# Local and coarse attention with a gated feed-forward: the late operand first in each group of TensorE products

## The chip, the core and the metric

The kernel runs on one core of one Trainium2 chip. The metric is device time in microseconds (us) of the program. The core's engines are TensorE (PE for its products, PEld for its weight loads), VectorE (DVE), ScalarE (ACT), GpSimd (POOL) and SyncE (SP, which only issues transfers). Every engine runs its own queue in the order of the program, and semaphores tie the queues together.

## The reference

Inputs are q, k and v of 8 batches, 8 heads, 576 positions and 64 numbers a head. Two attentions are added, and the sum goes through a normed, gated feed-forward:

```python
q_d, k_d, v_d = means of q, k, v over groups of 4 positions     # 144 coarse positions
out_up = repeat(softmax(q_d k_d^T / 8) v_d, 4)                  # coarse attention
out_local = softmax(q k^T / 8, only |i - j| < 4) v              # a band of 7
x = (out_up + out_local) as 4608 tokens of 512
xn = x / sqrt(mean(x * x) + 1e-6) * rms_g
g = xn @ w_gate;  val = xn @ w_val                              # 512 -> 1536
out = (g * sigmoid(g) * val) @ w_out                            # 1536 -> 512
```

## The kernel before

The tokens are cut into 18 chunks of 256, counted here from 0. For each chunk the local attention is made on VectorE, ScalarE and GpSimd, the coarse part is added, the rows are normed and transposed on TensorE (L906), and the feed-forward runs on TensorE. To keep float32 precision, every operand of the feed-forward is held as a high and a low part (xh and xl, hs[:, 0] and hs[:, 1], and two parts of each weight), and a product is three TensorE products: high by high, high by low, low by high.

The feed-forward of a chunk goes over 12 slices f of 128 hidden columns. `first(f, 0)` and `first(f, 1)` (L975) make the gate and the value product, 12 TensorE products of 256 columns each, into one buffer ps_h. Then follow tanh (ACT, L982), gate and product (DVE, L985 and L990), the high part of the result (ACT, L996) and the low part (DVE or POOL, L999). `second(f)` (L1010) makes six products of 512 columns into the two buffers ps_o; its place is two slices behind `first`. The parts that come last are xl (L914, after xh) for the first products of a chunk, and the low part of hs for every `second`.

The coarse attention is done in 32 pieces, a batch and a pair of heads each. A piece computes scores (four small products, L499; the two heads, par 0 and 1, lie in rows 0 to 63 and 64 to 127 of TensorE), row peaks on DVE, powers on ACT, a transposition of the powers (`turn`, L527, eight small transposes), their copy back (ACT, L534), the products with the values (`values`, L541, eight), and a store. All of the chunk's small TensorE outputs share three buffers, ps_a. The coarse keys, queries and values are summed from four parts by transfers that POOL issues one after another (L362), into two buffers each of qk and vs; the first part of vs is loaded by SP (L358) once the values of an earlier pair of pieces are done. Chunk 4 is the first that needs batches 2 and 3, whose last piece is made while chunk 3 runs.

Two things set the order. Up to the start of chunk 3 a planner in the kernel (class Plan, with costs and due times) writes the order of all engines out, as far as its own clock reaches the due time of chunk 3 plus 10 us; this part is issued under `manual_schedule`. What comes after is emitted in program order, and the scheduler of the language is free to move instructions: each engine takes the one that is ready first by the scheduler's own clock, with the earlier one preferred. So a group of products may be cut up there, its ready products placed early, and other work between them.

In the trace one product of `scores` or `values` (float32 operands) is two records; a product of L975 or L1010 and a transpose is one.

## Time and profile before

| | |
|---|---|
| median of three runs | 1149.9 us (1147.46 to 1150.06) |
| span of the profiled execution, first to last instruction | 1144.2 us |
| median less span | 5.7 us |
| TensorE products busy | 1082.0 us, 95% of the span |
| VectorE busy | 927.7 us, 81% |
| ScalarE busy | 624.1 us, 55% |
| GpSimd busy | 255.7 us, 22% |
| mean granted TensorE clock | 0.977 |

A row of the timeline has the start of a run of like instructions, the time that it covers, the engine, the line, out<-in with shapes, and the number of records; idle time before it and what ended it stand in brackets. TensorE's products overlap in the pipeline, so the cost of a run is read as its start to the start of the next row, not as its own length. A row of the windows view has, for each engine, busy time and instructions, then the granted TensorE clock, the share of the transfer engines and GB/s.

### The profile page before, as it was taken

The numbers are of one execution on the slowest core, as the hardware profiler recorded it, in microseconds if no ns is written. First come the engines' busy times: TensorE is split into PE (matmuls) and PEld (weight loads), VectorE is DVE, ScalarE is ACT, GpSimd is POOL, SyncE is SP. The second block draws the span as 40 slices with busy tenths as digits, with TensorE's granted clock in tenths as the row PEclk, the third lists the DMA queues.
The fourth block names the chain that finished last, engine by engine and source line by source line (L and its number), as shares of the span: only waits on it lengthen the run. The fifth ranks groups of instructions, "written<-read, shape, count | busy, mean of one in ns | idle before, by whom it ended". The sixth has DMA issues, their size and how long they took to land.

```text
span 1144.2 us, 22238 instructions
## 1 busy us (share of the span) xinstructions
PE 1082.0 (95%) x8002; PEld 990.2 (87%) x8002; DVE 927.7 (81%) x1869; ACT 624.1 (55%) x2284; POOL 255.7 (22%) x317
## 2 busy tenths in 40 slices
PE   6883799999999899999999999999999999999998
PEld 4772698888899899999999999999999999999997
DVE  6787898778889989797979797979798989887432
ACT  1574673747392847474747474747475573837221
POOL 1554562334221211111111111101011020201000
PEclk9885999999999999999999999999999999999999
DMA  9985482446535353535263535222231313220000
GB/s 264 301 275 170 102 227 76 95 101 149 127 87 117 99 115 88 115 87 115 83 120 87 115 88 114 78 64 75 66 91 46 105 52 99 68 58 20 1 19 19
DMA packets 76815, 119.59 MB, mean 105 GB/s; under 512 B 26784, under 2 KB 36256, under 8 KB 76704
## 3 DMA queue, kind: packets, MB, share of 16 engines
q1 hardware_dynamic: 47520, 97.34, 28.8%
q0 software_dynamic: 8640, 15.93, 9.0%
q10 hardware_dynamic: 20544, 4.89, 2.0%
q8 instruction: 63, 1.03, 0.4%
q14 instruction: 48, 0.39, 0.1%
HBM read 106.33 MB, written 11.80 MB: 103 GB/s over the span
## 4 chain that ended last, share of the span: by engine, by line
PE 76%; DVE 9%; DMA 8%; ACT 3%; issue 3%; SPq 1%; POOL 1%; ACTq 0%; DVEq 0%; POOLq 0%
PE ps_h L975 46%; PE ps_o L1010 23%; PE ps_a L541 2%; DMA wg<-in_v_sum_dram 2%; DMA qk<-in_qk_sum_dram 2%; PE ps_a L499 2%; ACT prod L804 1%; DMA vs<-in_v_sum_dram 1%; PE ps_a L906 1%; DVE prod L757 1%; DVE o_sb L271 1%; PE ps_a L527 1%; DMA kv<-in_k_pad_dram 1%; DVE sc L761 1%; DMA up<-o_g 1%
## 5 line engine op out<-in xcount | busy, mean ns | idle before, releaser
L1010 PE MATMUL ps_o<-wo,hs 128*128 128x512 f32 x1296 | 356.0, 399 | 4.2 <-POOL hs L999 3.7
L975 PE MATMUL ps_h<-xh,wg 128*128 128x256 f32 x1728 | 348.2, 283 | 4.8 <-ACT xh L910 2.3
L975 PE MATMUL ps_h<-xh,wv 128*128 128x256 f32 x1728 | 343.0, 281 | 4.6 <-DVE sil L985 4.5
L975 PEld LDWEIGHTS ps_h<-xh,wg 128*128 128x128 f32 x1728 | 282.9, 190 | 14.2 <-ACT xh L910 3.0
L975 PEld LDWEIGHTS ps_h<-xh,wv 128*128 128x128 f32 x1728 | 281.9, 189 | 10.8 <-DVE sil L985 6.9
L804 ACT ACTIVATE prod<-kv,sc 128x64 f32<-128x64 f32 x1072 | 281.7, 408 | 13.0 <-DVE sc L795 4.8
L1010 PEld LDWEIGHTS ps_o<-wo,hs 128*128 128x128 f32 x1296 | 221.9, 188 | 41.4 <-POOL hs L999 6.2
L975 PE MATMUL ps_h<-xl,wg 128*128 128x256 f32 x864 | 244.8, 283 | 0.1
L975 PE MATMUL ps_h<-xl,wv 128*128 128x256 f32 x864 | 241.5, 280 | 0.0
L982 ACT ACTIVATE sil<-ps_h 128x256 f32<-128x256 f32 x216 | 82.9, 384 | 233.9 <-PE ps_h L975 208.8
L811 POOL TENSOR_TENSOR prod<-sc,kv 128x256 f32<-128x256 f32 x144 | 116.4, 843 | 397.4 <-DVE sc L795 175.4
L985 DVE SCALAR_TENSOR_TENSOR sil<-sil,ps_h 128x256 f32<-128x256 f32 x216 | 89.7, 415 | 103.1 <-ACT sil L982 91.0
L975 PEld LDWEIGHTS ps_h<-xl,wg 128*128 128x128 f32 x864 | 164.1, 190 | 6.9 <-issue 1.3
L975 PEld LDWEIGHTS ps_h<-xl,wv 128*128 128x128 f32 x864 | 163.6, 189 | 1.8
L996 ACT ACTIVATE hs<-sil 128x256 fp32r<-128x256 f32 x216 | 89.5, 416 | 136.9 <-DVE sil L990 122.4
L757 DVE TENSOR_TENSOR prod<-q_t,kv 128x896 f32<-128x896 f32 x140 | 151.7, 1086 | 5.6 <-DMA q_t<-in_q_band_dram 5.2
L830 DVE TENSOR_REDUCE x_t<-prod 128x128 f32<-128x896 f32 x128 | 136.8, 1077 | 23.6 <-ACT prod L804 16.4
L761 DVE TENSOR_REDUCE sc<-prod 128x14 f32<-128x896 f32 x144 | 154.5, 1077 | 0.4
L999 DVE TENSOR_TENSOR hs<-sil,hs 128x256 fp32r<-128x256 f32 x196 | 91.4, 466 | 29.5 <-ACT hs L996 29.2
L990 DVE SCALAR_TENSOR_TENSOR sil<-sil,ps_h 128x256 f32<-128x256 f32 x216 | 89.9, 416 | 8.1 <-PE ps_h L975 6.4
L362 POOL DMA_DIRECT2D qk<-in_qk_sum_dram x36 | 32.2, 895 | 187.3 <-DMA qk<-in_qk_sum_dram 111.8
L811 DVE TENSOR_TENSOR prod<-sc,kv 128x128 f32<-128x128 f32 (+2 forms) x144 | 69.5, 515 | 1.6 <-PE ps_o L826 0.8
(118 smaller groups left out, 984.3 us busy)
## 6 DMA issues: line engine op xcount, KB each, us to landing
kv<-in_k_pad_dram SPq DMA_DIRECT2D x72, 320.0 KB
kv<-in_v_pad_dram SPq DMA_DIRECT2D x72, 320.0 KB
qk<-in_qk_sum_dram POOLq DMA_DIRECT2D x36, 288.0 KB, 5.3
out_dram<-o_sb SPq DMA_DIRECT2D x36, 256.0 KB
q_t<-in_q_band_dram SPq DMA_DIRECT2D x70, 128.0 KB
vs<-in_v_sum_dram POOLq DMA_DIRECT2D x36, 144.0 KB, 3.5
qk<-in_qk_sum_dram SPq DMA_DIRECT2D x12, 288.0 KB
wo<-in_qk_sum_dram SPq DMA_DIRECT2D x2, 1152.0 KB
```

The source lines that it names most:

```text
L757: nc.vector.tensor_tensor(out=pr, in0=bcast(q[:, s0:s0 + 2], 2, NO), in1=window(k, s0), op=ALU.mult)
L761: nc.vector.tensor_reduce(out=self.sc[:, j, par, s0:s0 + 2], in_=self.pr[i], axis=AX.X, op=ALU.add,)
L804: nc.scalar.activation(out=self.pr[i][:, o, s], in_=self.v[j, par][:, s0 + s + o], func=AF.Copy, scale=p[:, s, o:o + 1],)
L811: (nc.vector if engine == "DVE" else nc.gpsimd).tensor_tensor(out=self.pr[i][:, a:b], in0=bcast(p[:, :, a:b].rearrange("p s o -> p o s"), ...
L830: nc.vector.tensor_reduce(out=self.x[j][:, s0:s0 + 2, par], in_=pr.rearrange("p o s d -> p s d o"), axis=AX.X, op=ALU.add,)
L975: nc.tensor.matmul(out=self.p[f][:, t], lhsT=wi(f)[:, 0, k], rhs=xi[:, k], start=(n == 0), stop=(n == 3 * KT - 1),)
L982: nc.scalar.activation(out=self.sil[f], in_=self.p[f][:, 0], func=AF.Tanh, scale=0.5)
L985: nc.vector.scalar_tensor_tensor(out=self.sil[f], in0=self.sil[f], scalar=1.0, in1=self.p[f][:, 0], op0=ALU.add, op1=ALU.mult,)
L990: nc.vector.scalar_tensor_tensor(out=self.sil[f], in0=self.sil[f], scalar=0.5, in1=self.p[f][:, 1], op0=ALU.mult, op1=ALU.mult,)
L996: nc.scalar.activation(out=self.hs[f][:, 0], in_=self.sil[f], func=AF.Copy)
L999: (nc.gpsimd if engine == "POOL" else nc.vector).tensor_tensor(out=self.hs[f][:, 1], in0=self.sil[f], in1=self.hs[f][:, 0], op=ALU.subtract,)
L1010: nc.tensor.matmul(out=self.o[j], lhsT=lhs[:, cols], rhs=rhs(f)[:, 0], start=(f == 0 and i == 0), stop=(f == NF - 1 and i == 2),)
```

## The change

Within each group of TensorE products the order is turned so that the operand that is ready last is used first: xl ahead of xh in `first`, the low part of hs ahead of the high part in `second` (with the second half of the rows first, but for the last slice), the second head ahead of the first in `scores` and `turn`, and the second half of rows first in `turn`. The products and their sums are the same, in another order. In the part that the scheduler orders, each score product of a piece is also tied behind the one before it on TensorE (`issue_after`, an edge of order alone with no semaphore); in the written-out part it is not.

```diff
             def high():
                 self.invert()
-                for par in range(2):
+                for par in (1, 0):
                     self.turn(par)
                     self.copy(par)
...
+            last = None
             for c in range(2):
-                for par in range(2):
+                for par in (1, 0):
                     rows = slice(par * D, (par + 1) * D)
-                    nc.tensor.matmul(
-                        out=self.s[par][:, c], lhsT=qs[rows, hp % 2, c * HALF:(c + 1) * HALF], rhs=ks[rows, hp % 2],
-                        start=True, stop=True,
-                    )
+                    with tc.issue_after(last) if last and loose else nullcontext():
+                        last = nc.tensor.matmul(
+                            out=self.s[par][:, c], lhsT=qs[rows, hp % 2, c * HALF:(c + 1) * HALF], rhs=ks[rows, hp % 2],
+                            start=True, stop=True,
+                        ).ins
...
         def turn(self, par):
-            for kc in range(2):
-                for c in range(2):
+            for c in (1, 0):
+                for kc in range(2):
...
-                for wi, xi in ((w[0], self.att.xh), (w[0], self.att.xl), (w[1], self.att.xh)):
+                for wi, xi in ((w[0], self.att.xl), (w[0], self.att.xh), (w[1], self.att.xh)):
...
-            for j in range(2):
+            for j in (0, 1) if f == NF - 1 else (1, 0):
                 cols = slice(j * P, (j + 1) * P)
-                for i, (lhs, rhs) in enumerate(((hh, wo[0]), (hh, wo[1]), (hl, wo[0]))):
+                for i, (lhs, rhs) in enumerate(((hl, wo[0]), (hh, wo[0]), (hh, wo[1]))):
...
     with tc.manual_schedule():
         plan.run(due[FIRST] + 10)
+    loose.append(True)
     plan.run()
```

The lines shift by three or four: L499 becomes L502, L527 L530, L541 L544, L975 L978, L1010 L1013. The written-out part keeps its order of groups on every engine; in the rest the scheduler comes to another order, at three kinds of places above all. In the rows wo and wg stand for parts of the weights, hs for the hidden result, a_g for the powers of a coarse piece.

TensorE, the scores of one coarse piece in one of the chunks 6 to 11 (the same in each of the six). Before:

```order
L1010 MATMUL ps_o<-wo_2_1577,hs 128x512
L499 MATMUL ps_a<-qk 72x144 x2
L1010 MATMUL ps_o<-wo_2_1576,hs 128x512 x2
L975 MATMUL ps_h<-xh,wg_0_408 128x256
L499 MATMUL ps_a<-qk 72x144 x2
L975 MATMUL ps_h<-xl,wg_0_408 128x256
L975 MATMUL ps_h<-xh,wg_0_409 128x256
```

Now:

```order
L1013 MATMUL ps_o<-wo_1_1478,hs 128x512
L502 MATMUL ps_a<-qk 72x144
L1013 MATMUL ps_o<-wo_2_1576,hs 128x512 x2
L1013 MATMUL ps_o<-wo_2_1577,hs 128x512
L1013 MATMUL ps_o<-wo_2_1576,hs 128x512 x2
L1013 MATMUL ps_o<-wo_2_1577,hs 128x512
L502 MATMUL ps_a<-qk 72x144 x3
L978 MATMUL ps_h<-xl,wg_0_408 128x256
```

The piece was cut into two and two score products, and is cut into one and three. In two more pieces from chunk 4 on, two and two become four in a row.

TensorE, the transposes of the powers of one piece, in the same chunk. Before:

```order
L975 MATMUL ps_h<-xh,wg_0_408 128x256
L527 MATMUL ps_a<-ident_sb,a_g 72x72
L1010 MATMUL ps_o<-wo_2_1576,hs 128x512 x2
L527 MATMUL ps_a<-ident_sb,a_g 72x72 x4
L975 MATMUL ps_h<-xl,wg_0_408 128x256
L527 MATMUL ps_a<-ident_sb,a_g 72x72 x3
L975 MATMUL ps_h<-xh,wg_0_409 128x256
```

Now:

```order
L1013 MATMUL ps_o<-wo_2_1577,hs 128x512
L978 MATMUL ps_h<-xl,wv_0_415 128x256
L978 MATMUL ps_h<-xh,wv_0_415 128x256
L530 MATMUL ps_a<-ident_sb,a_g 72x72 x8
L978 MATMUL ps_h<-xh,wv_0_416 128x256
L978 MATMUL ps_h<-xl,wv_0_415 128x256
```

Eight transposes stand in one run. From chunk 4 on there were 41 runs of L527 for 16 pieces, and there are 16.

TensorE, the value products (L541, now L544) of a piece shortly before chunk 3, after which SP may load the next vs. Before:

```order
L1010 MATMUL ps_o<-wo_0_441,hs 128x512
L541 MATMUL ps_a<-vs,a_g 72x64 x4
L975 MATMUL ps_h<-xh,wg_1_1220 128x256
L975 MATMUL ps_h<-xl,wg_1_1220 128x256
L975 MATMUL ps_h<-xh,wg_1_1221 128x256
L541 MATMUL ps_a<-vs,a_g 72x64 x3
L1010 MATMUL ps_o<-wo_0_440,hs 128x512 x2
L541 MATMUL ps_a<-vs,a_g 72x64
```

Now:

```order
L1013 MATMUL ps_o<-wo_0_440,hs 128x512 x2
L1013 MATMUL ps_o<-wo_0_441,hs 128x512
L544 MATMUL ps_a<-vs,a_g 72x64 x8
L978 MATMUL ps_h<-xl,wg_1_1220 128x256
L978 MATMUL ps_h<-xh,wg_1_1220 128x256
L978 MATMUL ps_h<-xh,wg_1_1221 128x256
```

The eight value products stand together. Between the scores of the piece before and the last of these products, 75 products of L975 and 18 of L1010 stood before; now 72 and 12 do. On SP the load of vs (L358) moves from behind a load of q_t and one of kv to ahead of them. From chunk 4 on, the values of one piece in each of seven chunks are also followed at once by a piece's scores, with one product of L1010 between them before.

More of the change, by code (lines that the diff above doesn't have):

```diff
@@ L1 @@
 import itertools
-from contextlib import ExitStack
+from contextlib import ExitStack, nullcontext
 import concourse.bass as bass
@@ L431, in add_v @@
             )
+    loose = []
     used = {"wg": [], "wv": [], "wo": []}
```

## The prediction

> **What bounds the kernel now.** I read the page's busy shares first, then busy time by stretches, to see whether TensorE (PE) bounds every stage or an average hides one where it waits.
>
> ```profile
> span 1144.2 us, 22238 instructions
> ...
> L1010 PE MATMUL ps_o<-wo,hs 128*128 128x512 f32 x1296 | 356.0, 399 | 4.2 <-POOL hs L999 3.7
> ```
>
> ```profile
> 300.00:400.00 100.00, 95.80 (x707) 87.36 (x706) 88.57 (x180) 60.23 (x238) 23.97 (x37) 0.98 0.42 100
> 400.00:500.00 100.00, 100.00 (x753) 91.97 (x753) 86.44 (x189) 59.19 (x229) 21.25 (x27) 1.00 0.42 98
> 1000.00:1050.00 50.00, 50.00 (x363) 46.93 (x363) 44.07 (x95) 28.74 (x111) 5.73 (x8) 1.00 0.16 48
> ```
>
> The columns behind the first are PE, PEld, DVE, ACT and POOL, then the granted clock. From 400 us on PE has no idle time; the last two rows are the first and nearly the last such stretch. So there a wait can't be removed, only PE's own cost; DVE, at 86 to 88 of each 100, runs beside it with some room. Before 400 us PE idles a little and other chains set the starts of chunks. The same shows in the last row of the first fence: over the whole program PE waited 4.2 us ahead of its 1296 second products, so beginning such groups with the late operand has little to save.
>
> What a chunk of products costs is read from the chain of waits, where the last chunk repeats every 4.12 us:
>
> ```profile
> 1104.23 2.75 PE ps_h L975 x24
> 1108.35 2.75 PE ps_h L975 x24
> ```
>
> A slice is 24 products of 2.75/24 = 0.115 us and six of (4.12 - 2.75)/6 = 0.23 us. Between products of these two kinds a change costs nothing. Whatever a row takes beyond 0.115 and 0.23 us a product is the price of the small products between.
>
> **The change, part by part.** The number of products stays. What moves is where the small ones stand, so I price a break between kinds.
>
> Scores (PE's timeline; one piece cut into one and three, then one whole, then one cut into two and two):
>
> ```profile
> 327.27 0.46 PE L499 MATMUL ps_a<-qk 64*72 64x144 f32 x2
> 327.67 0.73 PE L541 MATMUL ps_a<-vs,a_g 72*72 72x64 f32 x8
> 328.33 0.71 PE L499 MATMUL ps_a<-qk 64*72 64x144 f32 x6
> 328.96 0.38 PE L975 MATMUL ps_h<-xh,wg 128*128 128x256 f32 x1
> ...
> 509.25 0.48 PE L1010 MATMUL ps_o<-wo,hs 128*128 128x512 f32 x1
> 509.66 0.71 PE L499 MATMUL ps_a<-qk 64*72 64x144 f32 x8
> 510.31 0.72 PE L1010 MATMUL ps_o<-wo,hs 128*128 128x512 f32 x2
> ...
> 547.54 0.85 PE L1010 MATMUL ps_o<-wo,hs 128*128 128x512 f32 x3
> 548.32 0.71 PE L499 MATMUL ps_a<-qk 64*72 64x144 f32 x4
> 548.96 0.73 PE L1010 MATMUL ps_o<-wo,hs 128*128 128x512 f32 x2
> 549.52 0.28 PE L975 MATMUL ps_h<-xh,wg 128*128 128x256 f32 x1
> 549.73 0.71 PE L499 MATMUL ps_a<-qk 64*72 64x144 f32 x4
> 550.37 0.39 PE L975 MATMUL ps_h<-xl,wg 128*128 128x256 f32 x1
> 550.59 0.40 PE L975 MATMUL ps_h<-xh,wg 128*128 128x256 f32 x2
> ```
>
> Half a piece takes 0.64 us from its start to the next row (548.32 to 548.96, 549.73 to 550.37), and a whole piece 0.65: the two heads run side by side when they alternate, and one after the other when each half is one head's. Around each run the product before takes about 0.09 us more (547.54 to 548.32 is 0.78 for three, against 0.69) and the one behind about 0.10 more (550.37 to 550.59 is 0.22). So two and two costs 2 x (0.64 + 0.19) = 1.66, whole 0.65 + 0.19 = 0.84. One and three is 0.40 + 0.63 with two such borders, 1.41. The order now has, from chunk 4 on, six pieces at one and three where two and two stood: 6 x 0.25 = 1.5 us. Of the two pieces that become whole, the one in chunk 5 gives 0.82; the one at the start of chunk 4 is told below. Sum 2.3 us. The bounds: a whole piece's price for the six (4.9 + 0.8 = 5.7 us), or the old price (0.8). I take 2.3, since one and three stands in the trace.
>
> Transposes:
>
> ```profile
> 385.82 0.66 PE L527 MATMUL ps_a<-ident_sb,a_g 72*72 72x72 f32 x8
> 386.29 0.36 PE L975 MATMUL ps_h<-xl,wg 128*128 128x256 f32 x1
> ...
> 558.57 0.41 PE L527 MATMUL ps_a<-ident_sb,a_g 72*72 72x72 f32 x4
> 558.79 0.36 PE L975 MATMUL ps_h<-xl,wg 128*128 128x256 f32 x1
> 558.99 0.35 PE L527 MATMUL ps_a<-ident_sb,a_g 72*72 72x72 f32 x3
> 559.15 0.36 PE L975 MATMUL ps_h<-xh,wg 128*128 128x256 f32 x1
> 559.35 0.28 PE L975 MATMUL ps_h<-xh,wv 128*128 128x256 f32 x1
> ```
>
> Four take 0.22 us, three 0.16, eight 0.47, and the product behind any run takes 0.20 instead of 0.115. If four and four replaced eight: 0.44 + one more 0.085, against 0.47, so a break costs 0.055 us. 41 runs become 16: 25 x 0.055 = 1.4 us. That the scores follow the values at once saves little: the lone L1010 at 509.25 took 0.41, 0.18 too much, and that goes, but a border between the two small kinds comes (0.09 on 327.67 to 328.33); 7 x 0.05 = 0.3. From chunk 4 to the end PE's work thus falls by 2.3 + 1.4 + 0.3 = 4.0 us.
>
> Late operand first, where PE does wait. At the start of chunk 4:
>
> ```profile
> 374.76 0.71 PE L499 MATMUL ps_a<-qk 64*72 64x144 f32 x4
> 377.08 0.62 PE L975 MATMUL ps_h<-xh,wg 128*128 128x256 f32 x3 [1.62 <-ACT xh L910]
> 378.26 0.68 PE L499 MATMUL ps_a<-qk 64*72 64x144 f32 x4 [0.56 <-DVE xl L914]
> 378.87 0.55 PE L975 MATMUL ps_h<-xl,wg 128*128 128x256 f32 x1
> ```
>
> Now all four scores need the buffer that xl's first half (DVE) frees at about 378.2, and the first L975 needs xl. Half the scores had run in idle time at 374.76, and three L975 at 377.08. The scores then take the same 0.6 us from 378.2, whole, and the three L975 come behind: 3 x 0.115, a loss of 0.3 us, and this piece's 0.82 is not gained. Behind the waiting products stands all of PE, but ACT and DVE work on the next values meanwhile. In the written-out part the groups that wait for the low part of hs lose the two products that ran ahead of it, 2 x 0.23 = 0.46 us each; the whole wait before L1010 there is the 4.2 us above, and later waits take such a shift up. I count zero, bound 0.9 (two groups). xl, needed one product earlier, costs 0.1 us at most elsewhere.
>
> The chain into chunk 3 (two rows of the chain of waits, then the norm on DVE's timeline):
>
> ```profile
> 293.44 0.14 PE ps_a L541 x2
> ...
> 293.59 4.49 DMA vs<-in_v_sum_dram
> ```
>
> ```profile
> 311.98 1.29 DVE L894 TENSOR_TENSOR x_t<-x_t,rinv 128x512 f32<-128x512 f32 x2 [2.63 <-POOL rinv L890]
> ```
>
> The last value products release SP's load of vs, POOL adds three parts behind it, each waiting for the one before, and only then makes the root that the norm of chunk 3 waits for. These value products now have 3 x 0.115 + 6 x 0.23 = 1.7 us less of products ahead of them and some breaks fewer, about 1.9 us. SP's q_t and kv move behind vs and are wanted later. DVE had idled 2.63 us here, so the norm can come 1.9 us earlier; PE meets it, as 4 fewer products (0.8 us) stand ahead of that transposition. Whether chunk 4 starts earlier by as much hangs on DVE's queue, which works between the two norms (its order there hardly changes), and on the values of the last piece of batch 3, which move some 2 us back. I take 1.5 of the 1.9; bounds 0 and 2.2.
>
> Sum: -4.0 + 0.3 - 1.5 = -5.2 us. The profiled span becomes 1144.2 - 5.2 = 1139.0, and as the median of the runs lies 5.7 us above the span, the time becomes 1149.9 - 5.2 = 1144.7 us.
>
> **A rule against it.** PE's clock fell to half at the start of chunk 4:
>
> ```profile
> 378.00:380.00 2.00, 1.74 (x9) 1.58 (x10) 1.59 (x3) 2.00 (x10) 0.01 (x1) 0.73 0.77 294
> 380.00:382.00 2.00, 2.00 (x12) 2.00 (x11) 2.00 (x5) 2.00 (x10) 1.01 (x1) 0.50 0.00 0
> 382.00:384.00 2.00, 2.00 (x17) 2.00 (x17) 1.97 (x4) 2.00 (x11) 1.20 (x1) 0.91 0.62 168
> ```
>
> That is 2 x (0.27 + 0.50 + 0.09) = 1.7 us lost after the idle time from 375 to 378. The change leaves PE with nothing between 374.8 and 378.2, so it will fall again; a second one, at chunk 3, would cost 1.7 us, and none at all would give 1.7 back. The Trainium skill, "TensorE: Matmul & The Clock Gate", Part 1 (The HAM clock gate), says that the clock halves after an idle window of some 3.4 us that runs freely, and comes back after a busy one. By that rule which gap is caught is a matter of phase; the trace agrees with the length, about 3.4 us between 378.9 and 382.4, as an estimate from the three rows.
>
> **The rivals.** (1) The forecast, 1144.7; its own range 1143 to 1146.4. 58%. (2) Chunk 4 follows early and the clock isn't halved, or the six cut pieces cost less: 1.7 to 2.4 us more, 1142.5. 9%. (3) PE's saving comes, but the early chain gives nothing and a second clock drop costs 1.7: -4.0 + 0.3 + 1.7 = -2.0, 1147.9. For it: the values of chunk 4's last piece come later. Against it: DVE's 2.63 us of idle time. 18%. (4) DVE sets the period of chunks 4 to 11, so that a shorter PE gains nothing: only chunk 3's 1.5 us less 0.3 remains, 1148.7. For it: 88.57 of 100 busy at 300 to 400; against it: PE without idle time in 400 to 500, where DVE idles 13.6. 9%. (5) Slower: a group that begins with the late operand holds all of PE, where two products (0.46 us) used to run ahead of the low part of hs. It decides once 11 groups lose 0.46 (5.2 us) and 19 make it slower by over 0.3%; if one in four of the 168 groups from chunk 4 on did, 42 x 0.46 = 19.3 us, the time would be 1164. Against it stands the tail, where no other engine is late:
>
> ```profile
> 1131.80 0.38 ACT L982 ACTIVATE sil<-ps_h 128x256 f32<-128x256 f32 x1 [2.38 <-PE ps_h L975]
> 1133.57 0.42 DVE L999 TENSOR_TENSOR hs<-sil,hs 128x256 fp32r<-128x256 f32 x1 [0.48 <-ACT hs L996]
> ```
>
> From tanh to low part is 2.2 us, and the group stands two slices, 8.2 us, behind; DVE's backlog must reach 6 us. 4%. (6) The scores don't run side by side in the new order of heads: term one is lost, and ten whole pieces cost 0.4 more: 1144.7 + 2.3 + 4 = 1151. Against it: the six records of three at 328.33 take 0.63, as four of one head would. 2%.
>
> **How the numbers follow.** A measurement here tells about 0.3%, 3.4 us, from no change. Below 1146.5 lie (1), (2) and a little of (3): 0.70. Within: the rest of (3), (4) and most of (6): 0.25. Slower: (5) and a bad end of (6): 0.05. The range from 1140.5 to 1149.5 holds (1) to (4); its lower end is 1144.7 less 1.7 for the clock and 2.5 of the term of the scores, its upper end the case in which nothing but the transposes' 1.4 us is left, plus a us.
>
> **What would show it.** Scores in rows of x2 and x6 records at 0.4 and 0.63 us, transposes in rows of x8; the period of chunks 6 to 11 shorter by 0.5 us; PE without idle time from 400 us on; the norm of chunk 3 before 311 us and the first transposition of chunk 4 near 372. It is wrong if PE shows waits ahead of L1013 or L978 after 400 us, or if the norm of chunk 3 stays where it was.

## The result and the profile after

The changed kernel took 1139.6 us (median of four executions, 1136.23 to 1143.23), 0.9921 of the kernel before with a 95% interval of 0.9895 to 0.9947: 10.2 us less by the medians and 9.1 by the ratio, where 5.2 were forecast. The median lies 0.9 us below the lower end of the range; by the ratio the time is 0.9921 x 1149.9 = 1140.8 us, just inside it. A second comparison (experiment 10) gave 1139.88 us and 0.9933, 0.9905 to 0.9961. In one of the six executions of experiment 11 the mean granted clock was 0.559 in place of 0.970 to 0.974, and it took 1771.34 us; its ratio below is worked out from the other five.

The page and the stretches of the changed kernel, to be read as those of before:

```profile
span 1134.4 us, 22266 instructions
...
L1013 PE MATMUL ps_o<-wo,hs 128*128 128x512 f32 x1296 | 336.4, 396 | 7.2 <-POOL hs L1002 5.8
```

```profile
400.00:500.00 100.00, 100.00 (x773) 92.70 (x772) 88.41 (x195) 61.53 (x239) 22.89 (x27) 1.00 0.42 99
```

PE still has no idle time from 400 us on, but the stretch holds 773 records where it held 753. Ahead of the second products PE waits 7.2 us in place of 4.2, all of it before 314 us. The two profiled executions are fast ones of their kernels, with spans 5.7 and 5.2 us below the medians, so their difference can stand beside that of the medians.

To see where the time went, I take the first transposition of chunks 3, 6, 12 and 17 on PE's timeline. Before, then after:

```profile
312.81 1.23 PE L906 MATMUL ps_a<-ident_sb,x_t 128*128 128x128 f32 x8 [0.88 <-DVE x_t L894]
...
485.00 1.04 PE L906 MATMUL ps_a<-ident_sb,x_t 128*128 128x128 f32 x8
...
828.18 1.03 PE L906 MATMUL ps_a<-ident_sb,x_t 128*128 128x128 f32 x8
...
1082.60 1.04 PE L906 MATMUL ps_a<-ident_sb,x_t 128*128 128x128 f32 x8
```

```profile
311.51 1.04 PE L909 MATMUL ps_a<-ident_sb,x_t 128*128 128x128 f32 x8
...
480.71 1.04 PE L909 MATMUL ps_a<-ident_sb,x_t 128*128 128x128 f32 x8
...
819.35 1.03 PE L909 MATMUL ps_a<-ident_sb,x_t 128*128 128x128 f32 x8
...
1073.01 1.03 PE L909 MATMUL ps_a<-ident_sb,x_t 128*128 128x128 f32 x8
```

1.3 us are won up to chunk 3, 3.0 in chunks 3 to 5, 4.5 in chunks 6 to 11, 0.8 in chunks 12 to 16 and 0.2 behind, together the 9.8 us between the spans. The 0.8 is the surprise: chunks 12 to 16 hold no coarse piece, and PE has no idle time there.

The small products stand as the order said (scores of one piece, then transposes):

```profile
542.38 0.46 PE L502 MATMUL ps_a<-qk 64*72 64x144 f32 x2
542.77 1.66 PE L1013 MATMUL ps_o<-wo,hs 128*128 128x512 f32 x6
544.36 0.71 PE L502 MATMUL ps_a<-qk 64*72 64x144 f32 x6
545.00 0.38 PE L978 MATMUL ps_h<-xl,wg 128*128 128x256 f32 x1
...
553.87 0.66 PE L530 MATMUL ps_a<-ident_sb,a_g 72*72 72x72 f32 x8
```

One and three take 0.39 and 0.64 us. The norm of chunk 3, a piece of the chain of waits that leads to it, and the start of chunk 4 (before, then after):

```profile
310.15 1.29 DVE L897 TENSOR_TENSOR x_t<-x_t,rinv 128x512 f32<-128x512 f32 x2
```

```profile
305.39 0.09 DVE rinv L877
```

```profile
373.60 1.23 PE L906 MATMUL ps_a<-ident_sb,x_t 128*128 128x128 f32 x8 [0.74 <-DVE x_t L894]
```

```profile
371.71 0.46 PE L502 MATMUL ps_a<-qk 64*72 64x144 f32 x2
375.09 0.68 PE L502 MATMUL ps_a<-qk 64*72 64x144 f32 x6 [2.92 <-DVE xl L917]
```

```profile
376.00:378.00 2.00, 2.00 (x13) 2.00 (x12) 1.93 (x6) 2.00 (x11) 0.30 (x1) 0.59 0.05 18
378.00:380.00 2.00, 2.00 (x12) 2.00 (x11) 1.97 (x4) 2.00 (x11) 1.46 (x2) 0.55 0.52 134
```

The norm starts 1.8 us earlier (311.98 before), but not by the path that led to it before. There POOL gave out its last transfer of vs at 306.87 and began the root behind it at 307.70. Now that transfer goes out at 303.7, 3.2 us earlier, and the first step of the root on POOL (305.55) waits for a row of DVE, the 305.39 above. At chunk 4 the wait for the norm (0.74 us at 373.60) is gone; PE waits once, for xl, 2.92 us, and the clock falls afterwards as it did before: 2 x (0.41 + 0.45) = 1.7 us lost.

### The profile page after: what moved, and what is told of

Read it like the earlier page. It is cut to its first block, busy times and chain, and to the rows that moved or that the text cites. A ratio compares the mean times of both kernels' runs of the same rounds, so it can differ in the third digit from the quotient of the medians.

```text
span 1134.4 us, 22266 instructions
## 1 busy us (share of the span) xinstructions
PE 1067.8 (94%) x8002; PEld 982.7 (87%) x8002; DVE 921.6 (81%) x1869; ACT 622.5 (55%) x2284; POOL 261.3 (23%) x317
## 4 chain that ended last, share of the span: by engine, by line
PE 82%; DVE 7%; DMA 6%; issue 2%; ACT 2%; SPq 1%; POOL 1%; ACTq 0%; DVEq 0%; POOLq 0%
PE ps_h L978 49%; PE ps_o L1013 24%; PE ps_a L544 2%; DMA qk<-in_qk_sum_dram 2%; DMA wg<-in_v_sum_dram 2%; PE ps_a L502 2%; PE ps_a L909 1%; PE ps_a L530 1%; DVE prod L760 1%; DVE o_sb L271 1%; ACT up_t L858 1%; PE ps_o L829 1%; DVE sc L764 1%; SPq L396 1%; DVE wg L295 0%
## 5 line engine op out<-in xcount | busy, mean ns | idle before, releaser
L1013 PE MATMUL ps_o<-wo,hs 128*128 128x512 f32 x1296 | 336.4, 396 | 7.2 <-POOL hs L1002 5.8
L978 PE MATMUL ps_h<-xh,wg 128*128 128x256 f32 x1728 | 315.9, 279 | 1.7 <-DVE wg L295 1.7
L978 PE MATMUL ps_h<-xh,wv 128*128 128x256 f32 x1728 | 315.7, 279 | 0.0
L978 PEld LDWEIGHTS ps_h<-xh,wg 128*128 128x128 f32 x1728 | 266.9, 189 | 6.3 <-DVE wg L295 1.9
L1013 PEld LDWEIGHTS ps_o<-wo,hs 128*128 128x128 f32 x1296 | 228.4, 188 | 50.0 <-POOL hs L1002 8.0
L978 PEld LDWEIGHTS ps_h<-xh,wv 128*128 128x128 f32 x1728 | 266.7, 189 | 3.4
L978 PE MATMUL ps_h<-xl,wg 128*128 128x256 f32 x864 | 246.0, 285 | 1.7 <-DVE xl L917 1.4
L978 PE MATMUL ps_h<-xl,wv 128*128 128x256 f32 x864 | 242.7, 281 | 3.6 <-DVE sil L988 3.4
L814 POOL TENSOR_TENSOR prod<-sc,kv 128x256 f32<-128x256 f32 x144 | 119.0, 856 | 384.9 <-DVE sc L798 147.8
L978 PEld LDWEIGHTS ps_h<-xl,wv 128*128 128x128 f32 x864 | 163.6, 189 | 7.8 <-DVE sil L988 5.5
L978 PEld LDWEIGHTS ps_h<-xl,wg 128*128 128x128 f32 x864 | 163.5, 189 | 7.4 <-DVE xl L917 2.2
L1002 DVE TENSOR_TENSOR hs<-sil,hs 128x256 fp32r<-128x256 f32 x196 | 87.6, 448 | 21.2 <-ACT hs L999 20.9
```

The lines of the kernel that those rows point to most:

```text
L814: (nc.vector if engine == "DVE" else nc.gpsimd).tensor_tensor(out=self.pr[i][:, a:b], in0=bcast(p[:, :, a:b].rearrange("p s o -> p o s"), ...
L978: nc.tensor.matmul(out=self.p[f][:, t], lhsT=wi(f)[:, 0, k], rhs=xi[:, k], start=(n == 0), stop=(n == 3 * KT - 1),)
L1002: (nc.gpsimd if engine == "POOL" else nc.vector).tensor_tensor(out=self.hs[f][:, 1], in0=self.sil[f], in1=self.hs[f][:, 0], op=ALU.subtract,)
L1013: nc.tensor.matmul(out=self.o[j], lhsT=lhs[:, cols], rhs=rhs(f)[:, 0], start=(f == 0 and i == 0), stop=(f == NF - 1 and i == 2),)
```

## The experiments

Executions of one kernel differ by several us (the kernel before ran between 1142.6 and 1157.9 us beside these runs), but nearly all of that comes about before chunk 6, as far as three profiled executions of one order show (the change, experiments 8 and 10). So I read each run by parts. The table is worked out from the starts of PE's records: the time from the first transposition of chunk 0 to that of chunk 3, of chunk 3 to 6, 6 to 12 and 12 to 17; then for chunks 6 to 11 the mean distance from a 256-column product to the next product inside a run, and what is left of the stretch when 1728 and 432 products are taken off at their own mean distances (small products and borders).

| kernel | median us | ratio to before [95%] | 0-2 | 3-5 | 6-11 | 12-16 | distance ns | small, borders |
|---|---|---|---|---|---|---|---|---|
| before | | | 206.8 | 172.2 | 343.18 | 254.42 | 116.2 | 42.7 |
| the change | 1139.6 | 0.9921 [0.9895, 0.9947] | 204.6 | 169.2 | 338.64 | 253.66 | 115.3 | 39.9 |
| 1 coarse parts | 1142.5 | 0.9938 [0.9914, 0.9962] | 207.8 | 171.9 | 338.84 | 254.40 | 115.5 | 39.8 |
| 2 order of products | 1144.1 | 0.9954 [0.9935, 0.9973] | 211.0 | 172.3 | 339.21 | 253.67 | 114.4 | 41.9 |
| 3 free part only | 1139.5 | 0.9914 [0.9888, 0.9940] | 206.3 | 169.2 | 338.64 | 253.66 | 115.3 | 39.8 |
| 4 no queue of scores | 1142.8 | 0.9939 [0.9918, 0.9960] | 208.8 | 171.8 | 339.01 | 253.66 | 114.7 | 41.4 |
| 5 scores as a block | 1161.5 | 1.0124 [1.0099, 1.0148] | 206.6 | 183.5 | 344.35 | 253.66 | 114.7 | 46.7 |
| 6 xl first | 1148.6 | 0.9995 [0.9974, 1.0016] | 207.0 | 171.6 | 341.90 | 254.37 | 115.5 | 42.7 |
| 7 hl first | 1142.0 | 0.9964 [0.9943, 0.9985] | 209.2 | 171.8 | 339.05 | 253.77 | 114.4 | 41.9 |
| 8 the change's order, products alone behind it | | | 210.8 | 169.8 | 338.64 | 253.66 | 115.3 | 39.9 |
| 9 scores behind products | 1142.4 | 0.9960 [0.9938, 0.9982] | 212.0 | 171.2 | 335.04 | 253.66 | 115.3 | 36.4 |
| 10 the change again | 1139.9 | 0.9933 [0.9905, 0.9961] | 205.6 | 170.1 | 338.64 | 253.66 | 115.3 | 39.8 |
| 11 behind, from chunk 6 on | 1136.1 | 0.9875 [0.9840, 0.9911] | 205.6 | 169.9 | 335.04 | 253.66 | 115.3 | 36.3 |

### 1. The coarse parts alone

The changed kernel, with the products of L978 and L1013 in their old order:

```diff
-                for wi, xi in ((w[0], self.att.xl), (w[0], self.att.xh), (w[1], self.att.xh)):
+                for wi, xi in ((w[0], self.att.xh), (w[0], self.att.xl), (w[1], self.att.xh)):
...
-            for j in (0, 1) if f == NF - 1 else (1, 0):
+            for j in range(2):
-                for i, (lhs, rhs) in enumerate(((hl, wo[0]), (hh, wo[0]), (hh, wo[1]))):
+                for i, (lhs, rhs) in enumerate(((hh, wo[0]), (hh, wo[1]), (hl, wo[0]))):
```

> The change with the old order of products: only the coarse pieces' scores (second head first, queued behind each other) and their transpositions (rows outermost, second head first) are changed; L978's groups begin with xh and L1013's with hh as before. Theory A (the prediction: what is gained in chunks 6 to 11 are small products and their borders, and the small products do not need the new order of the groups): chunks 6 to 11 together 2.3 to 2.9 us shorter than before, the products' spacing inside a run at 116.2 ns as before, chunks 12 to 16 at 50.91 us each as before, the start of chunk 3 at 312.8 as before, and 1145.5 to 1146.5 us in all. Theory B (the shorter spacing of the products comes from calmer small products and not from the order in a group): also the spacing falls to about 115.3 ns, chunks 12 to 16 fall to 50.8, and the time is near 1143.5.

```profile
486.26 1.04 PE L909 MATMUL ps_a<-ident_sb,x_t 128*128 128x128 f32 x8
...
825.10 1.04 PE L909 MATMUL ps_a<-ident_sb,x_t 128*128 128x128 f32 x8
...
1079.51 1.04 PE L909 MATMUL ps_a<-ident_sb,x_t 128*128 128x128 f32 x8
```

Chunks 6 to 11 gave 4.3 us (343.18 to 338.84), more than A said; chunks 12 to 16 gave nothing, as A said. The small products and their borders account for 2.9, the size of A. The other 1.4 are the distance between products, 115.5 ns instead of 116.2, though no product inside a group was moved. So B holds where the small products changed, and only there: neither theory is whole. What became fewer are products at a longer distance behind transposes (the table in experiments 6 and 7). Chunks 3 to 5 hold a second drop of the clock here, 3.4 us at half from 316.4 us on, which costs 1.7 us.

### 2. The order of products alone

The kernel before with only the lines struck out in experiment 1.

> The kernel before with only the order inside the product groups changed: xl first in L975's, hl first in L1010's groups, second half first except in the last group. Scores and transpositions as before. Theory A (the gains add up by parts): the start of chunk 3 comes at about 311 and that of chunk 4 about 3 us earlier than before, chunks 6 to 11 win only what is left, the 1.7 us of the shorter product spacing, chunks 12 to 16 fall to 50.8 us, and the time is about 1143. Theory B (the spacing has nothing to do with the order): chunks 12 to 16 stay at 50.91, chunks 6 to 11 at 57.2, and only the start is won: about 1146.

```profile
488.10 1.04 PE L906 MATMUL ps_a<-ident_sb,x_t 128*128 128x128 f32 x8
...
827.31 1.03 PE L906 MATMUL ps_a<-ident_sb,x_t 128*128 128x128 f32 x8
...
1080.98 1.03 PE L906 MATMUL ps_a<-ident_sb,x_t 128*128 128x128 f32 x8
```

Chunks 12 to 16 fall to 253.67, the change's value to 0.01: that part of the gain belongs to the order of products, and B falls. But chunks 6 to 11 gave 4.0 us, and with experiment 1's 4.3 that is 8.3, where both together give 4.5. The parts don't add up. This one wins 3.2 us by the distance (114.4 ns) and 0.7 by borders; the change has more of the second and less of the first. The early start that A expected didn't come: chunk 3 began at 315.8, after 211.0 us from chunk 0. In this execution the clock fell three times between chunks 0 and 3 (at 134.1, 161.5 and 270.7 us), where it fell once in the kernel before; two more drops, each 3.4 us at half, are 3.4 us of that.

### 3. Late operand first in the free part only

```diff
-                for wi, xi in ((w[0], self.att.xl), (w[0], self.att.xh), (w[1], self.att.xh)):
+                for wi, xi in ((w[0], self.att.xl), (w[0], self.att.xh), (w[1], self.att.xh)) if loose else ((w[0], self.att.xh), (w[0], self.att.xl), (w[1], self.att.xh)):
```

and the same for L1013, with its order of halves.

> The changed kernel, but the groups of the written-out part (up to the start of chunk 3) keep the old order of products; the free part is as in the change. Theory A (the written-out groups lose because their late operand now stands first: by the trace 0.8 us from chunk 0 to chunk 1 and 0.3 left at chunk 2): the waits of L1013 for hs fall from 7.2 us to about 4, chunk 1 starts 0.8 us earlier against chunk 0 than in the change, and the time is 0.3 to 1.1 us lower, near 1139. Theory B (the loss is taken up by the waits for sums and weights before chunk 3): the waits move, chunk 3 starts at 311.5 as in the change and the time is that of the change, 1139.6.

The wait ahead of L1013 falls to 5.6 us. In five profiled executions with the late operand first in this part (the change, experiments 4, 8, 10 and 11) it is 7.2 to 10.1. But chunks 0 to 2 take 206.3 us against 204.6 to 210.8 in those five, and the medians can't be told apart (1139.5, and 1139.6 and 1139.9 for the change). That is theory B as far as the runs can tell: the waits of the written-out part move, and no time that shows in a median hangs on them; the 0.3 us at the lower end of theory A would not show.

### 4. Without the queue of the scores

```diff
-                    with tc.issue_after(last) if last and loose else nullcontext():
+                    with nullcontext():
```

> The changed kernel without the rule that a coarse piece's four score products are queued behind each other (the second head's half still stands first in the text). In this program 14 runs of two scores stand where the change has 7 pieces as one and three. Theory A (a piece of two and two costs 0.25 us more than one of one and three, as the prediction priced it): 7 x 0.25 = 1.8 us more than the change, chunks 6 to 11 longer by 1.5, 1141.3 in all. Theory B (the cut of the scores is not what was gained): within 0.5 us of the change.

One piece of chunk 7, now two and two, and the clock behind the start of chunk 4:

```profile
553.56 0.71 PE L502 MATMUL ps_a<-qk 64*72 64x144 f32 x4
554.20 1.67 PE L1013 MATMUL ps_o<-wo,hs 128*128 128x512 f32 x6
```

```profile
382.00:386.00 4.00, 1.62 (x6) 1.28 (x7) 3.17 (x7) 4.00 (x16) 1.58 (x2) 0.65 0.72 213
386.00:390.00 4.00, 4.00 (x21) 4.00 (x21) 3.90 (x8) 3.63 (x18) 1.95 (x2) 0.50 0.28 84
```

The halves take 0.64 each (the second from 555.80 to 556.43), and small products and borders in chunks 6 to 11 cost 1.6 us more, as the price of 0.25 a piece says. Yet the stretch is only 0.4 us longer, since the products run at 114.7 ns instead of 115.3 and give 1.2 us back. Chunks 3 to 5 lost 2.6 us, 1.7 of them to the clock, which stayed at half for twice as long (4 x 0.35 + 4 x 0.50 = 3.4 us lost); experiments 2, 7 and 9 show the same length, the change's order in four executions (the change, experiments 8, 10 and 11) never. This execution is the slowest of its ten (1147.83 us), so it doesn't show what lifts the median, 1142.8, above both theories. In chunks 6 to 11 it is theory B that came: 0.4 us.

### 5. The scores as one block

```diff
-            last = None
-            for c in range(2):
-                for par in (1, 0):
...
+            with tc.tile_critical() if loose else nullcontext():
+                for c in range(2):
+                    for par in (1, 0):
```

> The changed kernel with the four score products of a coarse piece made one block in the free part, in place of being queued behind each other: in this program all 18 pieces stand as four in a row (7 stood as one and three). Theory A (the price by runs: one and three 1.41 us, four in a row 0.84): 0.57 less for each of 7 pieces, chunks 6 to 11 together 3.4 us shorter than in the change (335.2), 1135.6 in all. Theory B (what the scores give is taken back by the products' spacing: where the queueing edge alone was taken out, small products cost 1.55 us more in chunks 6 to 11 but the products ran 1.2 us faster): chunks 6 to 11 about 337.5, the time 1138 to 1139.

```profile
617.96 0.71 PE L502 MATMUL ps_a<-qk 64*72 64x144 f32 x8 [1.16 <-POOL prod L814]
```

Slower by 14 us, and for reasons that neither theory had. The block waits for work on other engines: at 617.96 the scores wait 1.16 us for a local-attention product on POOL that they don't read, and at chunk 4 the block waited 6.0 us for one on ACT. And at the starts of chunks 3 and 4 the clock stayed at half for 10.2 us each (from 313.2 and 381.5 us), 10.2 us lost where the change loses 1.7. Nothing follows for the price of the scores; experiment 9 tried it again by order alone.

### 6 and 7. xl first alone, hl first alone

The two halves of experiment 2, each on the kernel before. Experiment 6, then experiment 7:

```diff
-                for wi, xi in ((w[0], self.att.xh), (w[0], self.att.xl), (w[1], self.att.xh)):
+                for wi, xi in ((w[0], self.att.xl), (w[0], self.att.xh), (w[1], self.att.xh)):
```

```diff
-            for j in range(2):
+            for j in (0, 1) if f == NF - 1 else (1, 0):
-                for i, (lhs, rhs) in enumerate(((hh, wo[0]), (hh, wo[1]), (hl, wo[0]))):
+                for i, (lhs, rhs) in enumerate(((hl, wo[0]), (hh, wo[0]), (hh, wo[1]))):
```

> The kernel before with xl first in L975's groups and nothing else. Its program has 72 switches from L1010 back to L975 in chunks 12 to 16 (81 before, 47 in the change) and 63 in chunks 6 to 11 (75 before). Theory A (the products' spacing is set by the number of such switches, each of which starts a stretch at 117 to 118 ns): chunks 12 to 16 stay near 50.88 us each, chunks 6 to 11 come to about 342.3 together, the time is 1147 to 1149. Theory B (the order of xh and xl inside the group sets the spacing): chunks 12 to 16 fall to 50.79, the time by 2 to 3 us.

> The kernel before with hl first in L1010's groups (and the second half first), nothing else. Its program has 51 switches from L1010 back to L975 in chunks 12 to 16 (81 before) and 48 in chunks 6 to 11 (75 before). Theory A (switches set the spacing): chunks 12 to 16 fall to 50.80 us, chunks 6 to 11 to about 339.5 together, and the time to about 1144.5. Theory B (the order inside L975's groups does it): chunks 12 to 16 stay at 50.91, chunks 6 to 11 win only the small products' borders, 0.7 us, and the time is 1147 to 1148.

Chunks 12 and 17 in experiment 6, then in experiment 7:

```profile
824.35 1.04 PE L906 MATMUL ps_a<-ident_sb,x_t 128*128 128x128 f32 x8
...
1078.72 1.03 PE L906 MATMUL ps_a<-ident_sb,x_t 128*128 128x128 f32 x8
```

```profile
824.91 1.04 PE L906 MATMUL ps_a<-ident_sb,x_t 128*128 128x128 f32 x8
...
1078.68 1.03 PE L906 MATMUL ps_a<-ident_sb,x_t 128*128 128x128 f32 x8
```

254.37 and 253.77 us, or 50.87 and 50.75 a chunk: xl first changes nothing there, hl first does nearly all, so theory B is out. Chunks 6 to 11 came to 341.90 and 339.05, near A's 342.3 and 339.5. With hl first, a group of L1010 has all it needs when its first product is ready, so the scheduler sets its six products in a row; with hh first it often sets two or four and goes back to L975. That is 81 switches from L1010 back to L975 in chunks 12 to 16 before, 72 with xl first, 51 with hl first, 47 in the change. xl first alone can't be told from no change (0.9995).

The number of switches goes with the distance only in chunks 12 to 16, though, and roughly there (72 switches gave no less than 81). The table below counts, from the starts of PE's records, the 256-column products that have 116 ns or more to the next one of their run, by what stands directly ahead of the run:

| kernel, chunks | all | behind L1010 | behind scores | behind transposes of powers | behind the rest | switches |
|---|---|---|---|---|---|---|
| before, 6 to 11 | 988 | 340 | 276 | 255 | 117 | 75 |
| 6 xl first, 6 to 11 | 744 | 365 | 12 | 251 | 116 | 63 |
| 7 hl first, 6 to 11 | 340 | 220 | 30 | 12 | 78 | 48 |
| 1 coarse parts, 6 to 11 | 702 | 357 | 276 | 30 | 39 | 81 |
| the change, 6 to 11 | 672 | 403 | 17 | 201 | 51 | 51 |
| before, 12 to 16 | 530 | 443 | | | 87 | 81 |
| 6 xl first, 12 to 16 | 541 | 453 | | | 88 | 72 |
| 7 hl first, 12 to 16 | 425 | 248 | | | 177 | 51 |
| the change, 12 to 16 | 427 | 252 | | | 175 | 47 |

In chunks 12 to 16 there are five or six such products for each switch in every order. In chunks 6 to 11 the change has more of them behind its switches than the kernel before; what it lost are long stretches behind the scores. Two such runs, before behind the scores at 549.73 (from 550.59 on, as the prediction shows it), and after behind those at 544.36:

```profile
556.13 1.09 PE L1010 MATMUL ps_o<-wo,hs 128*128 128x512 f32 x4
```

```profile
545.22 0.40 PE L978 MATMUL ps_h<-xh,wg 128*128 128x256 f32 x2
...
552.26 1.54 PE L1013 MATMUL ps_o<-wo,hs 128*128 128x512 f32 x6
```

Before, 47 products from 550.59 to 556.13 come every 118 ns; after, 62 from 545.22 to 552.26 every 113.5.

### 8. Products alone

Some 700 products behind the last chunk of the changed kernel, tied in one order:

```diff
+    probe_first(48)
+    for n in (6, 6, 6, 6, 12, 12, 12, 12, 2, 2, 4, 4):
+        probe_second(n)
+        probe_first(24)
+    for split in ((2, 2), (1, 3), (4,)):
+        for r in range(4):
+            for n in split:
+                probe_scores(n)
+                probe_first(12)
```

> The changed kernel with some 700 more products on TensorE behind the last chunk, when the other engines have nothing left to do; their results are thrown away, so the time in all means nothing and only their spacing is read. First 48 products as L978's, then runs of 6, 12, 2 and 4 like L1013's with 24 like L978's between them, then score products in runs of two and two, one and three, and four, with 12 like L978's between them. Theory A (a switch from L1013's to L978's form by itself starts the slower spacing): the first 3 to 24 products behind each switch come every 117 to 118 ns and the rest every 113.4, whatever the run's length, and the scores cost 1.66, 1.41 and 0.84 us for a piece as priced from the kernel before. Theory B (other engines' traffic makes the slower spacing): all products come every 113.4 ns, but for one border of 0.1 us, and the pieces of scores are cheaper than in the kernel.

DVE, ACT and POOL have nothing to do there:

```profile
1140.00:1160.00 20.00, 20.00 (x154) 19.02 (x153) 0.00 (x0) 0.00 (x0) 0.00 (x0) 1.00 0.02 9
```

Behind a run of six, then 24 products behind a run of four, that next run of four, and the products behind it (L1182 is like L978, L1188 like L1013):

```profile
1146.47 0.28 PE L1182 MATMUL ps_h<-xl,wg 128*128 128x256 f32 x1
...
1147.18 0.28 PE L1182 MATMUL ps_h<-xl,wg 128*128 128x256 f32 x1
...
1190.87 0.28 PE L1182 MATMUL ps_h<-xl,wg 128*128 128x256 f32 x1
...
1193.70 1.10 PE L1188 MATMUL ps_o<-wo,hs 128*128 128x512 f32 x4
1194.63 0.28 PE L1182 MATMUL ps_h<-xl,wg 128*128 128x256 f32 x1
...
1197.01 0.28 PE L1182 MATMUL ps_h<-xl,wg 128*128 128x256 f32 x1
```

The first six products behind a run of six take 0.71 us, 118 ns each on average (116 to 122 for five, then 113), and all later ones come every 113.3 ns. Behind the first run of four all 24 take 118 ns (2.83 us); behind the second, 21 take 2.38, 113.3 ns. Of the first 48 products, which follow scores, all but the first come at 113.3 ns. So the slower distance arises with DVE, ACT and POOL idle: theory B is out. It lasts for about five products or for the whole run, and which of the two it is, is not a matter of the run's length alone. Nor does it need a switch from L1013's form, as theory A had it: of the 20 runs of 12 products behind scores, 6 came at 118 ns to their end (the one at 1215.84, for instance), and the others at 113.3 after at most four slower ones.

The pieces of scores (two of two and two, two of one and three, then four in a row; 12 products between any two):

```profile
1197.45 0.47 PE L1174 MATMUL ps_a<-o_sb 64*72 64x144 f32 x4
...
1201.39 0.47 PE L1174 MATMUL ps_a<-o_sb 64*72 64x144 f32 x4
...
1213.23 0.46 PE L1174 MATMUL ps_a<-o_sb 64*72 64x144 f32 x2
...
1217.45 0.46 PE L1174 MATMUL ps_a<-o_sb 64*72 64x144 f32 x2
...
1230.06 0.71 PE L1174 MATMUL ps_a<-o_sb 64*72 64x144 f32 x8
1232.32 0.71 PE L1174 MATMUL ps_a<-o_sb 64*72 64x144 f32 x8
```

Less 24 or 12 products of 0.1133: two and two cost 3.94 - 2.72 = 1.22 us, one and three 1.50, four in a row 0.90 (1.48 and 0.85 where the products behind come at 113.3). The last two agree with the 1.41 and 0.84 of the prediction. Two and two is cheaper here than the 1.66 it cost in the kernel, since here each pair holds both heads, which run side by side (0.40 a pair), where the scheduler's halves were one head's (0.64).

### 9. The scores behind the products that cut them

The L1013 group between one and three was written ahead of the scores. An edge of order alone sets the first score product behind it:

```diff
-            last = None
+            last = behind[0]
...
-                    nc.tensor.matmul(
+                    behind[:] = [nc.tensor.matmul(
                         out=self.o[j], lhsT=lhs[:, cols], rhs=rhs(f)[:, 0],
                         start=(f == 0 and i == 0), stop=(f == NF - 1 and i == 2),
-                    )
+                    ).ins]
```

> The changed kernel, in whose free part a coarse piece's first score product is also queued behind the L1013 group written last before it, the one that cut the pieces into one and three. In this program 17 pieces stand as four in a row and 2 as one and three (11 and 7 in the change), and every piece of chunks 6 to 11 as four. Price by the products alone: a piece as one and three 1.45 us, as four 0.86, so 0.59 less for each of 6 pieces in chunks 6 to 11. Theory A (the products' spacing stays): chunks 6 to 11 together 335.1 us (338.64 in the change), the time 3 to 4 us below the change's. Theory B (part is taken back by more products in the slower spacing, as when the queueing edge was taken out): chunks 6 to 11 between 336 and 338, the time 1 to 2 us below the change's.

A piece of chunk 7, a wait in chunk 2, and the same wait in experiment 8 (L1014 is L1013 there), whose order is the change's:

```profile
550.15 0.71 PE L502 MATMUL ps_a<-qk 64*72 64x144 f32 x8
```

```profile
300.50 1.77 PE L1013 MATMUL ps_o<-wo,hs 128*128 128x512 f32 x5 [2.95 <-POOL hs L1002]
```

```profile
301.09 2.70 PE L1014 MATMUL ps_o<-wo,hs 128*128 128x512 f32 x6 [2.44 <-POOL hs L1003]
```

In chunks 6 to 11 theory A came true to 0.1 us: 335.04, 3.6 less than the change, at the same distance of 115.3 ns. And yet the median lies 2.5 us above the change's in the same comparison (0.9960 for 0.9933; the intervals overlap). The edge also moved the first free piece, in chunk 2, and others up to chunk 5. In the profiled execution one group in chunk 2 waited 2.95 us for the low part of hs from POOL, the clock halved (0.50 granted from 302 to 304 us), and chunks 0 to 2 took 212.0 us instead of 205. That the moved piece made this wait is not shown: experiment 8 has such a wait of 2.44 us at the same place without the edge, the clock at half from 301.4 us on, and 210.8 us for chunks 0 to 2.

### 10. The change again

> The changed kernel once more, beside the run above and the kernel before. Theory A (from chunk 3 on an execution repeats itself, and what differs between executions lies before it): chunks 6 to 11 again 338.6 us together, chunks 12 to 16 again 50.79 each, while the start of chunk 3 moves by a microsecond or more; the median near 1139.6, 0.991 to 0.992 of the kernel before. Theory B (the spacing of the products differs from execution to execution): chunks 6 to 11 off by more than 0.5 us.

338.64 and 253.66 us for chunks 6 to 11 and 12 to 16, to the hundredth what they were; chunks 0 to 2 differed by 1.0 us and chunks 3 to 5 by 0.9. In experiment 8, a third execution of this order, they are 338.64 and 253.66 again, and chunks 0 to 2 differ by 6.2 us, 3.4 of them by two more drops of the clock than in the change. So theory A holds, and with it the right to read differences of 0.1 us from chunk 6 on.

### 11. Behind, but only from chunk 6 on

```diff
-            last = behind[0]
+            last = behind[0] if len(loose) > 1 else None
...
+        if c == 6:
+            loose.append(True)
```

> As in the run before with the scores behind L1013's last written group, but only for pieces written from chunk 6 on: up to there the program is that of the change, from there every piece stands as four in a row. In the run before, chunks 6 to 11 won the 3.6 us of the price, but the rule also moved a piece in chunk 2, where L1013 then waited 3.2 us for hs and the clock fell for 3.4 us. Theory A (that loss came from the moved piece alone): chunks 0 to 5 as in the change within its spread, chunks 6 to 11 about 335.1 us together, the time 3 to 4 us below the change's, near 1136, 0.989 to 0.991 of the kernel before. Theory B (the time won is given back later in any case): the time within 1 us of the change's, 0.993.

```profile
483.73 1.04 PE L909 MATMUL ps_a<-ident_sb,x_t 128*128 128x128 f32 x8
...
818.77 1.03 PE L909 MATMUL ps_a<-ident_sb,x_t 128*128 128x128 f32 x8
```

335.04 us again, with the start of the change: 1136.1 us, 0.9875 of the kernel before (0.9840 to 0.9911). The median is 3.8 us below that of the change in experiment 10, but that was another comparison, and the two intervals just overlap; what shows the gain over the change is the 3.6 us of the trace. The price of the scores stands. From experiment 9 (0.9938 to 0.9982) the intervals lie apart, and the two programs differ only in what comes before chunk 6, so what experiment 9 lost was lost by the edge there; by which wait is open.

## Why the prediction was right or wrong, point by point

By the two profiled executions, in us (waits without the product that precedes them; the four L1010 moved behind the start of chunk 3 are set back). In chunks 3 to 5 the split between small products and distance is sure to 0.3 us only, as products at half clock lie in it.

| term | predicted | measured |
|---|---|---|
| up to the start of chunk 4, with the waits there | -1.5 + 0.3 | -0.8 |
| small products and borders, chunks 3 to 5 | -1.1 | -2.2 |
| the same, chunks 6 to 11 | -2.9 | -2.8 |
| distance between products, all chunks from 3 on | 0 | -4.0 |
| sum | -5.2 | -9.8 |

- **What bounds the kernel**: right. PE has no idle time from 400 us on, and each us that PE was spared there came off the time, in experiment 11 as well. The period of chunks 6 to 11 fell by 0.76 us, where 0.5 was forecast. DVE, rival (4), sets no period: chunks 6 to 11 could still be shortened by 3.6 us.
- **"Between products of these two kinds a change costs nothing"** is the step that failed, and with it the border that was priced on one product behind a run. It makes up nearly all of the difference (4.0 of 4.6 us). It was read from the last chunk, whose 24 and six products repeat evenly. In its place the runs showed that behind a switch from L1010 to L975, or behind a run of small products, the next products can come at 118 ns instead of 113.3, for some five of them or for the whole run (experiment 8). The share of 256-column products at 116 ns or more fell from 62% to 42% in chunks 6 to 11 and from 40% to 31% in chunks 12 to 16. In chunks 12 to 16 it fell with the number of switches, 47 for 81, and hl first does that (experiment 7). In chunks 6 to 11 it was the stretches behind the scores that went (17 products for 276), while behind switches there are 403 for 340. What decides how long a stretch lasts stays open.
- **The range**: that the time came out within a us of its lower end is luck. That end was put there for a clock that isn't halved and for cheaper scores, and neither came; the time got there by a term that stood at nothing.
- **Scores**: right in size. One and three at 0.39 and 0.64 us, 0.25 cheaper than two and two by head, which experiment 4 confirms in the small products (1.6 us for six pieces); four in a row 0.6 cheaper again (experiment 11: 3.6 us for six). But the price of a cut was not the price in time: without the queue the products gave 1.2 of 1.6 us back by their distance.
- **Transposes**: the eight stand in one row. With the scores they make the 2.8 us; they were not tried apart.
- **Chunks 3 to 5**: under-sized by 1.1 us in small products; where in these chunks it lies was not tried.
- **Late operand first at chunk 4's start**: the wait for xl came as described, one of 2.92 us. The clock fell once more for the same 1.7 us, so the rival in which it doesn't was wrong, and the Trainium skill's rule ("TensorE: Matmul & The Clock Gate", Part 1) agrees with the length. What was not foreseen is that the wait for the norm ahead of chunk 4's first transposition went too (0.74 us by its row, 0.9 from start to start).
- **Written-out part, counted as zero, bound 0.9**: right for the time as far as can be told. The waits themselves rose by more than the bound, from 4.2 to 7.2 us, but putting the old order back there (experiment 3) won nothing that shows.
- **The chain into chunk 3**: the norm came 1.8 us earlier, near the forecast 1.9, and PE no longer waited for it, in four executions of this order. But the agreement of the two numbers is luck. POOL was through with vs 3.2 us earlier, not 1.9, and then DVE's own row came last. With the parts alone PE still waited in experiments 1, 2 and 7, not in 6. How much of the time this is worth stays unsure, since chunks 0 to 2 took 204.6 to 210.8 us in four executions of the change's order.
- **Rival (3)** did not come. A second drop of the clock at chunk 3 is real, though: experiment 1 had one. In experiments 2, 4, 7 and 9 the drop at chunk 4 lasted twice as long instead, which costs as much. **Rival (5)**, groups from chunk 4 on that hold PE for the low part, did not come: the change shows no wait ahead of L1013 there. Ahead of chunk 3 there are such waits, up to 1.5 us in the change and 3.1 in experiment 10. **Rival (6)** was wrong: the heads run side by side.

## What to carry to other kernels

Where an engine has no idle time, look for what a like instruction costs in different places: here the same product took 113 or 118 ns by what stood ahead of it, and no wait showed it. Here an order that lets a group run through at once was worth more than the wait that it was meant to avoid. Price a break between kinds in a probe behind the program, and look at more than the first product behind it. And let an edge that wins in the steady part begin only there: set on the early pieces too, the same edge took back the 3.6 us that it won later.

## What the runs showed of the hardware

- There are two distances between like products on TensorE, 113.3 and 117 to 119 ns for 256 columns, also with DVE, ACT and POOL idle (experiment 8). The slower one begins at a switch from 512-column products or behind small products, and ends after some five products or lasts to the end of the run. What decides between the two is open. The Trainium skill's formula for the isolated gap ("TensorE: Matmul & The Clock Gate", Part 2, Back-to-back issue gap) gives 109 ns as an estimate for 256 columns; both measured distances lie above it.
- A run of score products in rows of 64 costs 0.20 us at its two borders beside its own time (the product ahead takes 206 instead of 113 ns by the starts of experiment 8, the one behind 222). The Trainium skill ("TensorEngine Tiling (Array Packing)", Key Properties) says that a change of tiling mode drains TensorE. The trace agrees with a cost of that kind but doesn't single it out: the product behind the transposes, which lie in 72 rows, takes 200 ns too.
- After the wait for xl at chunk 4 the clock stayed at half for 3.4 us or for 6.8, and the longer time did not go with the longer wait. From the product before the wait to the one behind it were 3.0 to 3.1 us in experiments 2, 4 and 9 (6.8 us at half), 3.1 in experiment 6 (3.4 us), and 3.2 to 3.35 in the change and experiments 3, 8, 10 and 11 (3.4 us).
